# Products of q, k, v and gate for token blocks 1 to 3 over 64 rows, each row group in its own order of tiles, with another lead, first block and end

## The chip, the cores and the metric

The kernel runs on one core of a Trainium2 chip. Five engines with queues of their own take part: TensorE (in the profile PE, its weight loads PEld), VectorE (DVE), ScalarE (ACT), GpSimd (POOL) and SyncE (SP, which here only issues DMAs). The metric is device time in microseconds (us) of one launch; lower is better.

## The reference

The input x has 2048 tokens of 640 features. The output mixes two sublayers by a gate of each token: a Fourier mixing over features and tokens, and an attention with 32 query heads of 20 features and one head of keys and values (MQA). Everything is float32.

```python
a = einsum("bsd,ed->bse", x, dft_hid_re)
b = einsum("bsd,ed->bse", x, dft_hid_im)
y = einsum("ts,bse->bte", dft_seq_re, a) - einsum("ts,bse->bte", dft_seq_im, b)
q = heads(x @ wq)          # 32 heads of 20
k, v = x @ wk, x @ wv      # one head
o = softmax(q @ k.T * 20 ** -0.5) @ v
g = sigmoid((x * gate_w).sum(-1))
out = g * y + (1 - g) * (o @ wo)
```

## The kernel before

**Precision.** A float32 operand is split into a high part of type fp32r (by ACT) and the rest as a low part (by DVE or POOL). A product is three: high by high, high by low, low by high (`mm3`, L120).

**First stage, L347 to L503.** Tokens come in four blocks of 512, transposed: x is 640 rows, in five chunks of 128. `split_x1(n, c)` (L371) makes xh and xl of block n, chunk c, by one ACT and one DVE instruction. For each block five q tiles of 128 rows (m) take 15 products each (5 chunks by 3 terms, `q_mm`, L381), and one tile for k, v and the gate takes ten (`kv_mm`, L395): 85 products of 128 rows and 512 columns. `q_out` (L386) evicts a q tile: qh by ACT, ql by DVE, two DMAs on SP's queue to `qh_d` and `ql_d`. Its buffers qh and ql have three places each. `kv_out` (L402) evicts k and v: kvl by ACT, kvT by DVE, kh by ACT, kl by DVE, and six DMAs by POOL's queue into `ks`. `kv_turn` (L417) transposes kvT on TensorE into `vsb` and `gz`. `load_qs0` (L156) reads q of the first pair of heads back from HBM into `qs[0]`, by SP's queue.

Block 0 goes chunk by chunk as its data lands, with all six sums open (L438 to L456). Then stand the splits of block 1 (L460), the evictions of block 0 (L461 to L463) and the loads of block 2. Blocks 1 to 3 (L469 to L503) go tile by tile, and after 13 of the q tiles (`slots`) stand four a products.

**a, b and av.** For each pair of heads an a product (`a_unit`, L243) of 60 rows gives scores of 128 queries by 512 keys; DVE reduces each to a row maximum (L258). Two a products, one of each head, lie on rows 0 to 59 and 64 to 123 (`hh`), so that they can run side by side. `a_final` (L277) writes the negated maxima to HBM and reads them back into rows 60 and 61 of `qs`, after so many steps of a clock that `tick` counts (`later`). A b product of 62 rows (`b_unit`, L968) then gives scores less the maximum, transposed; ACT takes the exponential (pt), and `av_step` (L985) sums pt with v and a column of ones, in bank V.

**Lead and main loop.** `f_stream` gives the products of the Fourier part, 64 rows at a time; `Halves` (L779) keeps one queue for each half of the rows. The lead (from L1086) runs 120 of its steps, with a products spread over them until 40 pairs are done. Then plans, written out by hand, interleave Fourier steps (y0, y1), a, b, evictions (E) and av (V). The first plan, FIRST (L1084), has four more b products than AB15, just ahead of its two V: b products are one step ahead of av from there on.

**End.** `finish_last` (L1014) evicts the last av sums, spreads the softmax sums over the rows with a product by `spread`, takes the reciprocals, scales and splits. `begin_late` (L752) begins the output products of the last token tile with the chunks that are ready; `o_group` (L758) does the rest, and one DMA for each of the last eight token tiles stores 320 KB.

**Order.** TensorE, ACT, DVE and POOL run their instructions as the program lists them (`manual_schedule`); only SP's are put in order by the framework. A DMA that ACT or POOL issues stands in that engine's order.

## Time and profile before

| | us |
|---|---|
| median of 3 runs | 1720.98 (1719.69 to 1721.21) |
| the profiled execution | 1719.39 |
| its span | 1717.6 |
| PE busy | 1705.2 (99%) |
| DVE busy | 1380.8 (80%) |
| ACT busy | 1251.4 (73%) |
| POOL busy | 1117.4 (65%) |

The profile has one execution, instruction by instruction. Its span goes from the first to the last instruction of the program; 1.8 us of the execution's time lie around it. A row of the timeline has the start, the duration, the engine, the line, the operation, what is written and read, and, where the engine was idle ahead of it, for how long and what ended that. A matmul's duration includes the way through the array, so that back-to-back matmuls overlap; their starts tell the pace. Rows of a merged run of like instructions have their count (x5) and the time from the first start to the last end.

### The profile page before, as it was taken

The page shows a single profiled execution, that of the slowest core. Times are in us where ns is not written, and L with a number is a line of the kernel's source. Part 1 is how long each engine was busy: PE and PEld are TensorE (multiplying, and loading weights), DVE is VectorE, ACT ScalarE, POOL GpSimd, SP SyncE. Part 2 cuts the span into 40 slices and gives each one's busy share as a digit, 9 for nine tenths or more (in the row PEclk, how much of TensorE's full clock was granted, in tenths as well). Part 3 has the DMA queues.
Part 4 walks back from the last instruction along what each step waited for, and adds up shares of the span by engine and source line. Part 5 has one row for each costly group of instructions (what it writes and reads, how often), then busy time and mean ns, then how long its engine had stood idle before and what let it go on. Part 6 is the DMA issues. An engine that isn't in the chain of part 4 may idle for free.

```text
span 1717.6 us, 43365 instructions
## 1 busy us (share of the span) xinstructions
PE 1705.2 (99%) x16754; PEld 1235.0 (72%) x16754; DVE 1380.8 (80%) x2294; ACT 1251.4 (73%) x2547; POOL 1117.4 (65%) x947
## 2 busy tenths in 40 slices
PE   9999999999999999999999999999999999999998
PEld 7686777777777777777777777777777777777665
DVE  5788888888888888888888888888888888888823
ACT  4247888888776777777777777777777767678896
POOL 2354556332366568758767888888877765547786
PEclk9999999999999999999999999999999999999999
DMA  8641223222265546546666776655555533143332
GB/s 283 187 140 48 73 83 105 76 78 74 78 218 168 190 150 210 161 148 216 219 219 205 236 234 232 193 191 181 178 174 170 155 114 114 52 128 111 108 92 97
DMA packets 180394, 261.47 MB, mean 152 GB/s; under 512 B 35856, under 2 KB 134416, under 8 KB 180188
## 3 DMA queue, kind: packets, MB, share of 16 engines
q1 hardware_dynamic: 179420, 257.71, 46.9%
q8 instruction: 132, 2.16, 0.5%
q0 software_dynamic: 768, 0.99, 0.3%
q14 instruction: 74, 0.61, 0.1%
HBM read 184.42 MB, written 76.99 MB: 152 GB/s over the span
## 4 chain that ended last, share of the span: by engine, by line
PE 98%; ACT 1%; DVE 1%; issue 0%; DMA 0%; POOL 0%; SPq 0%; DVEq 0%; ACTq 0%
PE av L983 27%; PE y_p L791 21%; PE b L971 19%; PE a L251 15%; PE ab L791 7%; PE oo L791 3%; PE q L122 1%; PE q L124 1%; PE q L123 1%; PE kv L400 1%; ACT pt L979 1%; DMA wraw<-in_wq_dram 0%; DVE pt L1028 0%; DVE osp L1034 0%; POOL tb L808 0%
## 5 line engine op out<-in xcount | busy, mean ns | idle before, releaser
L258 DVE TENSOR_REDUCE mx<-a 128x1 f32<-128x512 f32 x2048 | 1304.4, 686 | 242.7 <-PE a L251 190.2
L979 ACT ACTIVATE pt<-b 128x512 f32<-128x512 f32 x2048 | 1058.0, 623 | 342.4 <-PE a L251 255.9
L971 PE MATMUL b<-qs,ks 62*128 62x512 f32 x2048 | 756.8, 408 | 1.9 <-ACT pt L979 1.4
L251 PE MATMUL a<-ks,qs 60*128 60x512 f32 x2048 | 703.4, 407 | 1.3 <-DVE mx L258 1.3
L791 PE MATMUL y_p<-tb,ch 64*128 64x320 f32 x3584 | 618.4, 307 | 0.0
L791 PEld LDWEIGHTS y_p<-tb,ch 64*128 64x128 f32 x3584 | 504.8, 186 | 3.0
L983 PE MATMUL av<-pt,vsb 128*32 128x512 f32 x4096 | 484.9, 597 | 0.0
L971 PEld LDWEIGHTS b<-qs,ks 62*128 62x128 f32 x2048 | 346.2, 184 | 186.4 <-DVE mx L258 124.7
L791 PE MATMUL y_p<-tb,cl 64*128 64x320 f32 x1792 | 455.0, 306 | 0.0
L251 PEld LDWEIGHTS a<-ks,qs 60*128 60x128 f32 x2048 | 345.0, 185 | 14.5 <-issue 3.2
L791 PEld LDWEIGHTS y_p<-tb,cl 64*128 64x128 f32 x1792 | 297.2, 185 | 2.6
L983 PEld LDWEIGHTS av<-pt,vsb 128*32 128x32 f32 x4096 | 111.4, 109 | 239.6 <-issue 230.0
L551 POOL TENSOR_TENSOR cl<-craw,ch 128x1024 fp32r<-128x1024 f32 x112 | 268.5, 2397 | 9.0
L833 POOL TENSOR_TENSOR yt<-yt,yu 128x320 f32<-128x320 f32 x86 | 75.0, 872 | 291.0 <-ACT yu L828 257.3
L833 POOL TENSOR_TENSOR abt<-abt,abu 128x320 f32<-128x320 f32 x64 | 55.8, 871 | 194.9 <-ACT abu L828 176.7
L545 POOL TENSOR_TENSOR craw<-craw 128x1024 f32<-128x1024 f32 x64 | 153.6, 2399 | 0.0
L550 POOL CAST ch<-craw 128x1024 fp32r<-128x1024 f32 x112 | 116.5, 1040 | 6.4 <-PE ab L791 2.3
L791 PE MATMUL oo<-wo,osp 64*128 64x320 f32 x816 | 91.6, 306 | 0.0
L791 PEld LDWEIGHTS oo<-wo,osp 64*128 64x128 f32 x816 | 86.5, 185 | 1.6
L577 POOL TENSOR_TENSOR tb<-braw,tb 128x320 fp32r<-128x320 f32 x80 | 69.8, 878 | 0.0
L791 PE MATMUL ab<-wbh,xh 64*128 64x320 f32 x256 | 59.5, 307 | 0.0
L791 PE MATMUL ab<-wbh,xl 64*128 64x320 f32 x256 | 59.4, 305 | 0.0
(140 smaller groups left out, 1619.8 us busy)
## 6 DMA issues: line engine op xcount, KB each, us to landing
craw<-in_cre_dram SPq DMA_DIRECT2D x80, 512.0 KB
craw<-in_cim_dram SPq DMA_DIRECT2D x64, 512.0 KB
s_d<-craw SPq DMA_DIRECT2D x32, 512.0 KB
craw<-s_d SPq DMA_DIRECT2D x32, 512.0 KB
braw<-b_d SPq DMA_DIRECT2D x80, 160.0 KB
xraw<-in_xT_dram SPq DMA_DIRECT2D x32, 320.0 KB
b_d<-abt SPq DMA_DIRECT2D x64, 160.0 KB
t_d<-braw SPq DMA_DIRECT2D x64, 160.0 KB
```

The source lines that it names most:

```text
L122: nc.tensor.matmul(ps, wh, xh, start=(i == 0), stop=False)
L251: nc.tensor.matmul(ps, qs[v][b : b + 60, qb * P : (qb + 1) * P], ks[b : b + 60, c * ROW : (c + 1) * ROW], start=True, stop=True,)
L258: nc.vector.tensor_reduce(mx[v][:, hh, qb, c : c + 1], ps, axis=AX.X, op=ALU.max)
L545: nc.gpsimd.tensor_tensor(x, raw[0], x, op=how)
L550: nc.gpsimd.tensor_copy(h, x)
L551: nc.gpsimd.tensor_tensor(l, x, h.bitcast(F32), op=ALU.subtract)
L577: nc.gpsimd.tensor_tensor(t[:, 1], raw, t[:, 0].bitcast(F32), op=ALU.subtract)
L791: nc.tensor.matmul(ps, w, x, start=start, stop=stop)
L833: nc.gpsimd.tensor_tensor(t0, t0, t1, op=ALU.add)
L971: nc.tensor.matmul(ps, ks[b : b + 62, kc * P : (kc + 1) * P], qs[NPAIR * (qc // 2) + p][b : b + 62, (qc % 2) * ROW : (qc % 2 + 1) * ROW], ...
L979: nc.scalar.activation(t, ps, AF.Exp, scale=SCALE)
L983: nc.tensor.matmul(ps[32 * g : 32 * g + 32, :], vsb[:, kc, :], t, start=first, stop=last)
```

## The change

- **Blocks 1 to 3.** Each product of 128 rows becomes two of 64 rows, on rows 0 to 63 and 64 to 127 (`RG`). Both halves add into the same bank, but at different times: rows 0 to 63 go through the tiles as kv, q1, q0, q2, q3, q4, rows 64 to 127 as q0, kv, q3, q4, q1, q2. `Tile.run` issues one product. When a tile's first half is complete, ACT copies one column of its last weights onto itself, and the tile's second half, which runs through the products in reverse, starts with those weights. When the tile is complete it is evicted in place. Loads, splits and transposes stand at numbered steps (`event`). Pairs of a stand at 30 steps, in place of 13 groups of four products. Low parts of x of blocks 2 and 3 are made by POOL.
- **First block.** The first chunk of wq comes in two pieces by ACT's DMA queue. The k/v products run a chunk behind q, and each tile is evicted when its last product has been issued.
- **qs[0].** For blocks 0 and 1 the first q tile is copied into `qs[0]` straight from qh and ql by six DMAs of POOL's queue; `load_qs0` is gone.
- **Lead.** a products start eight steps later; four b products stand at steps 102 to 117, in bank V; the first plan is AB15. The maxima come back after 3 ticks instead of 5 in this stage.
- **End.** The sums are turned by small products, inverted as 8 columns in place of 256, widened, and spread by products with the identity; `begin_late` is cut in pieces between these. The last token tile is stored in two halves, one by SP, one by ACT.

The old body of `finish_last` and the old loop over blocks 1 to 3 are in the listing above and are left out here.

```diff
-    spread = const.tile([P, P], F32, name="spread")
-    for g in range(0, P, 32):
-        nc.gpsimd.tensor_copy(spread[:, g : g + 32], ident[:, g + DH : g + DH + 1].to_broadcast([P, 32]))
...
-    def load_qs0(n):
-        if n == 0:
-            qs[0] = qbuf[0]
-        ts = slice(n * ROW, (n + 1) * ROW)
-        for hh in range(2):
-            r = slice(hh * DH, (hh + 1) * DH)
-            for k, src in enumerate((qh_d, qh_d, ql_d)):
-                b = 64 * hh + 20 * k
-                move(qs[0][b : b + 20, ts], src[r, ts])
...
-            later(5, move, qs[v][r : r + 2], m_d[v][:, hh * QB : (hh + 1) * QB].rearrange("i b g t -> i (b g t)"))
+            later(5 if stage["loop"] else 3, move, qs[v][r : r + 2], m_d[v][:, hh * QB : (hh + 1) * QB].rearrange("i b g t -> i (b g t)"))
...
-                nc.vector.tensor_tensor(xl[:, c], xs[n, c], xh[:, c].bitcast(F32), op=ALU.subtract)
-
-        def q_mm(ps, n, m, c):
+                low = nc.vector if n < 2 else nc.gpsimd
+                low.tensor_tensor(xl[:, c], xs[n, c], xh[:, c].bitcast(F32), op=ALU.subtract)
+
+        def q_ops(n, m):
             ms = slice(m * P, (m + 1) * P)
+            return [(P, w[:, c, ms], x[:, c]) for c in range(KC) for w, x in q_terms(n)]
+
+        def q_terms(n):
             xh, xl = xsp[n]
-            mm3(ps, wqh[:, c, ms], wql[:, c, ms], xh[:, c], xl[:, c], KC, c)
+            return (wqh, xh), (wqh, xl), (wql, xh)
+
+        def kv_ops(n):
+            xh, xl = xsp[n]
+            ops = [[(105, kvgs[:, c, :105], xh[:, c]), (41, kvgs[:, c, :41], xl[:, c])] for c in range(KC)]
+            ops[-1].reverse()
+            return sum(ops, [])
+
+        class Tile:
+
+            def __init__(self, ops, name, out):
+                self.ops, self.name, self.out = ops, name, out
+                self.ps, self.made = None, 0
+
+            def run(self, rows, i):
+                if self.ps is None:
+                    self.ps = rots[0](self.name)
+                if rows is not None and self.made >= len(self.ops):
+                    i = len(self.ops) - 1 - i
+                m, w, x = self.ops[i]
+                n = len(self.ops) if rows is None else 2 * len(self.ops)
+                self.made += 1
+                r = slice(0, P) if rows is None else RG[rows]
+                nc.tensor.matmul(self.ps[:m], w[r], x[r], start=self.made == 1, stop=self.made == n)
+                if self.made == n:
+                    self.out(self.ps)
+                elif rows is not None and self.made == len(self.ops):
+                    nc.scalar.activation(w[:, :1], words(w[:, :1]), AF.Copy)
+
+        def q_tile(n, m):
+            return Tile(q_ops(n, m), f"q_{n}_{m}", lambda ps: q_out(ps, n, m))
+
+        def kv_tile(n):
+            return Tile(kv_ops(n), f"kv_{n}", lambda ps: kv_out(ps, n))
 
         def q_out(ps, n, m):
...
+            if m == 0 and n < 2:
+                if n == 0:
+                    qs[0] = qbuf[0]
+                for hh in range(2):
+                    for k, src in enumerate((qh, qh, ql)):
+                        b = 64 * hh + 20 * k
+                        nc.gpsimd.dma_start(words(qs[0][b : b + 20, ts]), words(src[hh * DH : (hh + 1) * DH]))
...
-            return kvT
+            kvTs[n] = kvT
...
+        kvTs = {}
+        arot = Rot(["S2", "S3", "S4"])
+
         load_x1(0, 0)
-        move(kvg, wkvg.rearrange("(c p) n -> p c n", p=P))
-        pkv = rot("kv_0")
-        pq = [rot(f"q_0_{m}") for m in range(KC)]
-        for c in range(KC):
-            if c:
-                load_x1(0, c)
+        cut = 2 * P
+        pieces = (slice(0, cut), slice(cut, D))
+        raw0 = w1.tile([P, D], F32, name="wraw", bufs=2)
+        for cs in pieces:
+            nc.scalar.dma_start(raw0[:, cs], wq_v[:, 0, cs])
+        split_x1(0, 0)
+        for cs in pieces:
+            split(raw0[:, cs], wqh[:, 0, cs], wql[:, 0, cs])
+        for c in range(1, KC):
+            load_x1(0, c)
             raw = raw_tile([P, D], "wraw") if c in (2, 3) else w1.tile([P, D], F32, name="wraw", bufs=2)
             move(raw, wq_v[:, c])
-            if c == 0:
+            if c == 1:
+                move(kvg, wkvg.rearrange("(c p) n -> p c n", p=P))
+            split_x1(0, c)
+            split(raw, wqh[:, c], wql[:, c])
+            if c == 1:
                 nc.vector.tensor_copy(kvgs[:, :, :41], kvg)
                 nc.vector.tensor_tensor(
                     kvgs[:, :, 64:105], kvg, kvgs[:, :, :41].bitcast(F32), op=ALU.subtract
                 )
-            split_x1(0, c)
-            split(raw, wqh[:, c], wql[:, c])
-            kv_mm(pkv, 0, c)
-            for m in range(KC):
-                q_mm(pq[m], 0, m, c)
+        rots = [rot]
+        tkv = kv_tile(0)
+        tq = [q_tile(0, m) for m in range(KC)]
+        order = [[(k, m) for m in range(KC) for k in range(3)] for c in range(KC)]
+        order[0] = [(0, 0), (0, 1), (1, 0), (1, 1), (0, 2), (0, 3), (0, 4), (2, 0), (2, 1), (1, 2), (1, 3), (1, 4)]
+        order[0] += [(2, 2), (2, 3), (2, 4)]
+        for c in range(KC):
+            ops = [(t, 3 * c + k) for k, m in order[c] for t in tq[m : m + 1]]
+            kv = [(tkv, i) for i in range(max(0, 2 * c - 2), 2 * c + 2 if c == KC - 1 else 2 * c)]
+            for t, i in kv[:2] + ops[:6] + kv[2:] + ops[6:]:
+                t.run(None, i)
         for c in range(KC):
             load_x1(1, c)
         for c in range(KC):
             split_x1(1, c)
-        kvT = kv_out(pkv, 0)
-        for m in range(KC):
-            q_out(pq[m], 0, m)
         for c in range(KC):
             load_x1(2, c)
-        load_qs0(0)
...
+        rots[0] = Rot(["F1", "V", "S0", "F0", "S1"])
+        at = {}
+
+        def event(k, f, *args):
+            at.setdefault(k, []).append((f, args))
+
+        NB = 17 * KC
         for n in range(1, 4):
+            s0 = (n - 1) * NB
+            for c in range(KC):
+                if n == 1:
+                    event(s0, load_x1, 3, c)
+                if n < 3:
+                    event(s0 + 12 + 14 * c, split_x1, n + 1, c)
             if n > 1:
+                event(s0, lambda n=n: load_w(n - 2, 0, x1.tile([P, KC, ROW], F32, tag="xr", name="wraw")))
+                event(s0 + 40, split_w, n - 2)
+            event(s0 + 50, kv_turn, n)
+        s0 = 2 * NB
+        for k in range(2):
+            event(s0 + 25, load_x, k)
+            event(s0 + 55 + 15 * k, split_x, k)
+        event(s0 + 70, load_x, 2)
+        event(32, kv_turn, 0)
+        event(s0 + 50, gate_out)
+        slots = [40 + 7 * k for k in range(24)] + [220 + 6 * k for k in range(6)]
+
+        for n in range(1, 4):
+            ts = [kv_tile(n)] + [q_tile(n, m) for m in (1, 0, 2, 3, 4)]
+            rows = [[(ts[z], i) for z in x for i in range(len(ts[z].ops))] for x in (range(6), (2, 0, 4, 5, 1, 3))]
+            for i, both in enumerate(zip(*rows, strict=True)):
+                k = NB * (n - 1) + i
+                for f, args in at.pop(k, ()):
+                    f(*args)
+                if k in slots:
+                    for hh in range(2):
+                        a_half(hh, arot.tags[arot.n % 3])
+                        arot.n += 1
+                for r, (t, j) in enumerate(both):
+                    t.run(r, j)
+        assert not at
...
-    def begin_late(e):
-        ps = begun[NT - 1, e] = bank(f"S{e}", f"o_late{e}")[:, :HALF]
+    def begin_late(e, c0, c1):
+        if c0 == 0:
+            begun[NT - 1, e] = bank(f"S{e}", f"o_late{e}")[:, :HALF]
+        ps = begun[NT - 1, e]
         h, l = osp[NT - 1]
-        for c in range(OC):
+        for c in range(c0, c1):
             mm3(ps, h[:, c], l[:, c], *wos[c, e], OC + 1, c)
 
...
+        if tb == NT - 1:
+            at = (nc.sync, nc.scalar)[e]
+            at.dma_start(out[tb * P : (tb + 1) * P, e * HALF : (e + 1) * HALF], t)
+        elif e == 1:
             move(out[tb * P : (tb + 1) * P].rearrange("p (e n) -> p e n", e=2), acc[tb])
...
+        HC = ROW // 2
         a = av[1]
+        ob = [pp.tile([P, ROW], F32, name="pt")[:, :HC] for _ in range(2)]
+        on = [pp.tile([P, ROW], F32, name="pt")[:, :HC] for _ in range(2)]
+        rec = [op.tile([P, 16], F32, name="rc")[:, :8] for _ in range(2)]
+        wide = [pp.tile([P, ROW], F32, name="pt")[:, :HC] for _ in range(2)]
+        nc.scalar.activation(ob[0], a[:, :HC], AF.Copy)
+        nc.vector.tensor_copy(ob[1], a[:, HC:])
+        pick4 = ident.rearrange("p (g x) -> p g x", x=32)[:, :, DH]
+        for i in range(2):
+            ps = bank(f"S{3 + i}", f"turned{i}")
+            for c in range(2):
+                nc.tensor.matmul(ps[:, 4 * c : 4 * c + 4], ob[i][:, c * P : (c + 1) * P], pick4, start=True, stop=True)
+            nc.vector.reciprocal(rec[i], ps[:, :8])
+            nc.vector.tensor_copy(
+                wide[i].rearrange("p (k x) -> p k x", x=32),
+                rec[i].rearrange("p (k o) -> p k o", o=1).to_broadcast([P, 8, 32]),
+            )
+        begin_late(0, 0, 2)
         h, l = last_hl
+        for i, low in enumerate(((nc.vector, nc.gpsimd), (nc.vector, nc.vector))):
+            ps = bank("S2" if i == 0 else "V", f"wide{i}")
+            for c in range(2):
+                nc.tensor.matmul(ps[:, c * P : (c + 1) * P], wide[i][:, c * P : (c + 1) * P], ident, start=True, stop=True)
+            nc.vector.tensor_tensor(on[i], ob[i], ps[:, :HC], op=ALU.mult)
+            begin_late(0, 2 + i, 3 + i)
+        begin_late(1, 0, OC)
+        for i, low in enumerate(((nc.vector, nc.vector, nc.gpsimd, nc.gpsimd), (nc.vector, nc.vector, nc.gpsimd, nc.vector))):
+            cs = slice(i * HC, (i + 1) * HC)
             for j in range(2):
                 for g in NEW[j]:
+                    nc.scalar.activation(h[g : g + DH, j, cs], on[i][g : g + DH], AF.Copy)
+                for k, g in enumerate(NEW[j]):
+                    low[2 * j + k].tensor_tensor(
+                        l[g : g + DH, j, cs], on[i][g : g + DH], h[g : g + DH, j, cs].bitcast(F32), op=ALU.subtract
                     )
 
...
-    FIRST = AB15[:-2] + "b0S3 b1S0 b0S2 b1S3 V V".split()
-
     LEAD = 8
     NL = 2 * (UV + LEAD)
     KL = 15 * SJ
+    LATE = 8
+    EARLY_B = {102: (0, 0), 107: (1, 0), 112: (0, 1), 117: (1, 1)}
     done = first = 2 * state[0]
     for n in range(1, KL + 1):
         y_put(1)
         for g in range(2):
             halves.run(g)
-        while done < first + (NL - first) * n // KL:
+        while done < first + (NL - first) * max(0, n - LATE) // (KL - LATE):
             if done % 2 == 0:
                 tick()
             a_half(done % 2)
             done += 1
+        if n in EARLY_B:
+            hh, qc = EARLY_B[n]
+            b_unit(0, hh, 0, qc, "V")
...
-        yield FIRST
+        yield AB15
...
-    made = 0
-    old = []
+    made = 1
+    old = STEPS[:1]
...
-    for e in range(2):
-        begin_late(e)
```

More of the change, by code (lines that the diff above doesn't have):

```diff
@@ L393, in q_out @@
             move(ql_d[ms, ts], ql)
-        def kv_mm(ps, n, c):
-            xh, xl = xsp[n]
-            end = c == KC - 1
-            for high in (not end, end):
-                m, x = (105, xh) if high else (41, xl)
-                nc.tensor.matmul(ps[:m], kvgs[:, c, :m], x[:, c], start=(c == 0 and high), stop=(end and high))
+            if m == 0 and n < 2:
[5 more added lines that the diff above has]
+                        nc.gpsimd.dma_start(words(qs[0][b : b + 20, ts]), words(src[hh * DH : (hh + 1) * DH]))
         def kv_out(ps, n):
@@ L414, in kv_out, with kv_turn @@
                     nc.gpsimd.dma_start(words(ks[r0 + 20 * k : r0 + 20 * k + 20, ts]), words(src))
-            return kvT
-        def kv_turn(kvT, n, rot):
-            ps = rot(f"kvt_{n}")
+            kvTs[n] = kvT
+        def kv_turn(n):
+            kvT = kvTs.pop(n)
+            ps = arot(f"kvt_{n}")
             for j in range(4):
@@ L460 @@
             split_x1(1, c)
-        kvT = kv_out(pkv, 0)
-        for m in range(KC):
-            q_out(pq[m], 0, m)
         for c in range(KC):
             load_x1(2, c)
-        load_qs0(0)
-        rot = Rot(["F1", "V", "S0", "F0"])
-        slots = {1: (2, 3, 4), 2: range(KC), 3: range(KC)}
-        for n in range(1, 4):
-            if n == 1:
-                for c in range(KC):
-                    load_x1(3, c)
-            if n > 1:
-                load_w(n - 2, 0, x1.tile([P, KC, ROW], F32, tag="xr", name="wraw"))
-            pkv = rot(f"kv_{n}")
-            for c in range(KC):
-                kv_mm(pkv, n, c)
-            kvT, kvT0 = kv_out(pkv, n), kvT
-            if n == 3:
-                for k in range(2):
-                    load_x(k)
-            for m in range(KC):
-                ps = rot(f"q_{n}_{m}")
-                for c in range(KC):
-                    q_mm(ps, n, m, c)
-                split_x1(n + 1, m)
-                if n > 1 and m == 1:
-                    split_w(n - 2)
-                q_out(ps, n, m)
-                if (n, m) == (1, 0):
-                    load_qs0(1)
-                if m == slots[n][0]:
-                    kv_turn(kvT0, n - 1, rot)
-                if m in slots[n]:
-                    for z in range(4):
-                        a_half(z % 2, f"S{1 + z}")
-                if (n, m) == (3, 1):
-                    kv_turn(kvT, 3, rot)
-                    gate_out()
-                if n == 3 and m in (2, 3):
-                    split_x(m - 2)
-                if (n, m) == (3, 3):
-                    load_x(2)
@@ L1014, in finish_last @@
     def finish_last():
-        ob = op.tile([P, ROW], F32, name="ob")
-        cols = [slice(0, ROW // 2), slice(ROW // 2, ROW)]
+        HC = ROW // 2
         a = av[1]
-        nc.scalar.activation(ob[:, cols[0]], a[:, cols[0]], AF.Copy)
-        nc.vector.tensor_copy(ob[:, cols[1]], a[:, cols[1]])
-        sums = []
-        for i, cs in enumerate(cols):
-            sums.append(bank(f"S{2 + i}", f"sums{i}")[:, cs])
-            nc.tensor.matmul(sums[i], spread, ob[:, cs], start=True, stop=True)
@@ L1025, in finish_last @@
-        r, on = [pp.tile([P, ROW], F32, name="pt") for _ in range(2)]
-        h, l = last_hl
-        for cs, ps, low in zip(cols, sums, ((nc.vector, nc.gpsimd), (nc.vector, nc.vector))):
-            nc.vector.reciprocal(r[:, cs], ps)
-            nc.vector.tensor_tensor(on[:, cs], a[:, cs], r[:, cs], op=ALU.mult)
+        ob = [pp.tile([P, ROW], F32, name="pt")[:, :HC] for _ in range(2)]
+        on = [pp.tile([P, ROW], F32, name="pt")[:, :HC] for _ in range(2)]
+        rec = [op.tile([P, 16], F32, name="rc")[:, :8] for _ in range(2)]
@@ L1030, in finish_last @@
+        for i, low in enumerate(((nc.vector, nc.vector, nc.gpsimd, nc.gpsimd), (nc.vector, nc.vector, nc.gpsimd, nc.vector))):
+            cs = slice(i * HC, (i + 1) * HC)
             for j in range(2):
                 for g in NEW[j]:
-                    nc.scalar.activation(h[g : g + DH, j, cs], on[g : g + DH, cs], AF.Copy)
-                for g in NEW[j]:
-                    low[j].tensor_tensor(
-                        l[g : g + DH, j, cs], on[g : g + DH, cs], h[g : g + DH, j, cs].bitcast(F32), op=ALU.subtract
+                    nc.scalar.activation(h[g : g + DH, j, cs], on[i][g : g + DH], AF.Copy)
+                for k, g in enumerate(NEW[j]):
+                    low[2 * j + k].tensor_tensor(
+                        l[g : g + DH, j, cs], on[i][g : g + DH], h[g : g + DH, j, cs].bitcast(F32), op=ALU.subtract
```

1 line of the change is left out of this document (removed).

## Prediction

> **What bounds the kernel now.** I read the page's span and its chain of work first, then the busy time by stage, then the timeline of each seam between stages.
>
> ```profile
> span 1717.6 us, 43365 instructions
> ...
> PE 98%; ACT 1%; DVE 1%; issue 0%; DMA 0%; POOL 0%; SPq 0%; DVEq 0%; ACTq 0%
> ```
>
> The chain that ended last is TensorE's own work, so a change counts where it alters TensorE's work or makes it wait. The windows below hold: the first token block, blocks 1 to 3, the lead, the first plan up to its first av product, the main loop, and the end (each row: length; busy time and count of PE, PEld, DVE, ACT, POOL; granted clock; DMA share; GB/s).
>
> ```profile
> 5.94:26.39 20.45, 20.33 (x85) 15.54 (x86) 12.12 (x19) 11.05 (x19) 0.71 (x1) 1.00 0.95 318
> 26.39:98.13 71.74, 71.74 (x325) 50.80 (x324) 53.18 (x91) 21.13 (x41) 26.09 (x34) 1.00 0.65 208
> 98.13:120.90 22.77, 21.48 (x269) 20.95 (x266) 20.79 (x36) 10.20 (x25) 15.40 (x16) 1.00 0.42 134
> 120.90:128.69 7.79, 6.78 (x55) 4.64 (x51) 6.11 (x10) 6.97 (x16) 4.27 (x6) 1.00 0.27 86
> 128.69:1698.20 1569.51, 1568.52 (x15935) 1127.91 (x15934) 1275.49 (x2118) 1192.99 (x2433) 1059.63 (x871) 1.00 0.47 148
> 1698.20:1712.73 14.53, 12.24 (x76) 11.24 (x76) 11.55 (x20) 6.78 (x15) 6.82 (x9) 1.00 0.24 91
> ```
>
> The main loop, 1570 us, keeps its plans apart from the first, and starts with 40 pairs of a done in both kernels. The change is worth what the other stages give.
>
> **Blocks 1 to 3: what the row groups remove.** TensorE's timeline around one group of a products (start, duration):
>
> ```profile
> 44.02 0.39 PE L124 MATMUL q<-xh,wql 128*128 128x512 f32 x1
> 44.34 0.73 PE L251 MATMUL a<-ks,qs 60*128 60x512 f32 x4
> 45.00 0.50 PE L122 MATMUL q<-xh,wqh 128*128 128x512 f32 x1
> 45.34 0.39 PE L123 MATMUL q<-xl,wqh 128*128 128x512 f32 x1
> 45.57 0.40 PE L124 MATMUL q<-xh,wql 128*128 128x512 f32 x1
> ```
>
> Product follows product after 0.233 us (45.34 to 45.57). From 44.02 to 45.34 run one q product, two pairs of a over 64 rows side by side, and one q product: 4 x 0.233 = 0.93 us of work in 1.32. The other 0.39 lies in four starts 0.32 to 0.34 apart, two on each side of the change of shape. Thirteen such groups (52 a products) make 5.1 us. As a check, 255 products x 0.233 + 26 pairs x 0.233 + four sets of transposes of about 0.25 = 66.5 us, and the window has 71.7.
>
> After the change all products there use 64 rows, so nothing changes shape: **-5.1**. The products do not get cheaper: each matmul becomes two of 64 rows, which by the a pairs take one product's time. Thirty a pairs are placed there instead of 26: **+0.9**, which the lead gets back.
>
> The Trainium skill, "TensorE: Matmul & The Clock Gate", section "Part 1: The HAM clock gate", gives back-to-back products as N/2.4 GHz + 2.5 ns, 215.7 ns for 512 columns. This trace has 0.233 us at granted clock 1.00; were the page's figure to hold for the new pairs alone, an estimate of 255 x 0.017 = 4.3 us more would go. The trace has a duration for both shapes, so the sum uses 0.233.
>
> What is late next here is DVE, whose reduction frees the banks of the a products:
>
> ```profile
> L258 DVE TENSOR_REDUCE mx<-a 128x1 f32<-128x512 f32 x48 | 29.7, 680 | 0.0
> ```
>
> A pair costs two reductions, some 1.3 us. Now three banks rotate and a pair comes every 7 steps, 8 x 0.233 = 1.86 us; its second bank is the first bank of the pair before, free 1.15 us after that one's start. DVE may thus be 0.7 late. It is later where an eviction stands ahead of the reductions: at k/v of block 2 it waits for kvl (0.6), makes kvT (0.7), waits for kh (0.6), makes kl (0.7), about 2.4 us past its turn, so TensorE waits 1.7. At q0 of block 1 I get 0.35, at the pairs of q evictions 0.1 to 0.5 each, at the gate and the transposes together 0.8. Sum **+3.9** (bounds +1 and +6). The one-column ACT copies between a tile's halves find 5 steps or more (1.2 us) and cost nothing, unless ACT is that late.
>
> **The seam from block 0 to block 1: what is added.** Now block 1 starts without a gap:
>
> ```profile
> 26.16 0.40 PE L124 MATMUL q<-xh,wql 128*128 128x512 f32 x1
> 26.39 0.40 PE L400 MATMUL kv<-xh,kvgs 128*105 128x512 f32 x1
> ```
>
> It can, because x of block 1 was split long before, ahead of block 0's evictions on ACT and DVE, whose instructions run as the program lists them:
>
> ```profile
> 16.24 2.70 ACT L378 ACTIVATE xh<-xr 128x512 fp32r<-128x512 f32 x5
> ```
>
> ```profile
> 17.11 3.09 DVE L379 TENSOR_TENSOR xl<-xr,xh 128x512 fp32r<-128x512 f32 x5
> ```
>
> In the changed program a tile evicts itself when its last product is issued, so block 0's evictions come ahead of `split_x1(1, c)` (L460) on both queues. What these cost:
>
> ```profile
> 24.44 0.63 ACT L410 ACTIVATE kh<-kvT 20x512 fp32r<-20x512 f32 x1 [0.75 <-DVE kvT L409]
> 25.09 1.58 ACT L390 ACTIVATE qh<-q 128x512 fp32r<-128x512 f32 x3
> 28.67 0.60 ACT L390 ACTIVATE qh<-q 128x512 fp32r<-128x512 f32 x1 [2.00 <-PE kv L400]
> ```
>
> The fourth qh waits here although its product is long done: qh has three buffers, and the first is still being written out, by the SP DMA below, 25.72 to 28.67. After the change that buffer is also read by POOL's copies into qs[0], six in place of `load_qs0`:
>
> ```profile
> 25.72 0.82 SPq L114 DMA_DIRECT2D qh_d<-qh  x2
> ```
>
> ```profile
> 25.68 0.73 POOL L414 DMA_DIRECT2D ks<-kh  x1 [20.77 <-ACT qh L390]
> 26.41 0.52 POOL L414 DMA_DIRECT2D ks<-kl  x1
> ```
>
> ```profile
> ks<-kh POOLq DMA_DIRECT2D x16, 40.0 KB, 3.2
> ks<-kl POOLq DMA_DIRECT2D x8, 40.0 KB, 4.0
> ```
>
> Let E be the time at which block 1 could start. q0's last product is 15 products before E: its sum is out at E-3.1, qh0 at E-2.5. POOL issues six copies at about 0.5 each from E-2.2; the fifth, the last that reads qh0, at E-0.1, landing 3.2 to 4.0 later, near E+3.5; the sixth reads ql0, is issued at E+0.4 and lands near E+4.4. Then ACT: qh3, qh4, five xh at 0.54 (2.70/5). DVE: ql3 from about E+4.6, ql4, five xl at 0.61 (3.09/5), the last done at E+8.9. Block 1's k/v tile uses one chunk of x every two steps; its step 8 needs the last xl and could run at E+1.9 (8 x 0.233). So TensorE is late by **+7.1**. If the buffers were free at once, kh, kl, the three evictions and the splits alone give E+5.9, +4.1: the lower bound. Behind POOL's copies stand block 0's k/v copies, needed only by the a products at step 40. An idle stretch of 5 us brings the clock in:
>
> ```profile
> 1712.70:1715.30 2.60, 0.03 (x1) 0.00 (x0) 0.72 (x2) 0.00 (x0) 0.28 (x1) 1.00 1.02 390
> 1715.40:1717.60 2.20, 0.00 (x0) 0.00 (x0) 0.00 (x0) 0.00 (x0) 0.00 (x0) 0.50 0.33 127
> ```
>
> 2.6 us after the last product the granted clock is 0.50. Most of a slow stretch would hide behind DVE's 0.61 per chunk; I take **+0.5** (0 to 2).
>
> **Start and block 0.** Now ACT waits for x, then for all of wq's first chunk:
>
> ```profile
> 2.01 0.22 ACT L108 ACTIVATE gate<-ident 128x16 f32<-128x16 f32 x1
> 4.45 0.63 ACT L378 ACTIVATE xh<-xr 128x512 fp32r<-128x512 f32 x1 [2.22 <-DMA xr<-in_xT_dram]
> 5.75 0.74 ACT L117 ACTIVATE wqh<-wraw 128x640 fp32r<-128x640 f32 x1 [0.67 <-DMA wraw<-in_wq_dram]
> ```
>
> After, two pieces come by ACT's queue, issued after 2.23; the first, 128 KB, should land between 5.0 and 6.2, so the first product starts near 5.65 and later pieces cost some 0.7. Against 5.94 with 20.45 - 85 x 0.233 = 0.65 of waits: **-0.4** (-1.2 to +0.6). Dropping `spread` frees POOL, which nobody waits for.
>
> **Lead and first plan.** The lead's first wait and the end of the first plan:
>
> ```profile
> 100.29 0.49 PE L251 MATMUL a<-ks,qs 60*128 60x512 f32 x1 [1.26 <-DVE mx L258]
> ```
>
> ```profile
> 126.15 1.48 PE L971 MATMUL b<-qs,ks 62*128 62x512 f32 x3
> 128.27 0.49 PE L971 MATMUL b<-qs,ks 62*128 62x512 f32 x1 [0.65 <-ACT pt L979]
> 128.69 1.92 PE L983 MATMUL av<-pt,vsb 128*32 128x512 f32 x16
> ```
>
> The a wait (1.5) goes, as `LATE` holds a back, but the lead's first sum now lies in S0, which block 3's last q tile gives up only after ql: 1.45. Together **0**. Ten a pairs instead of 14: **-0.9**. The four b products at the end, 2.5 us paced by ACT, move into the lead; there they cost 0.5 of TensorE, and, all in bank V behind an ACT that is 45% busy (10.20 of 22.77) and itself waits for evictions, some 1.0 of waiting: **-1.0** (-2.2 to +0.5). The shorter delay of the maxima's write-back, 3 ticks, leaves the DMA over 8 us before the first b.
>
> **End.**
>
> ```profile
> 1698.63 1.16 PE L1024 MATMUL sums<-ob,spread 128*128 128x256 f32 x4 [0.47 <-ACT ob L1019]
> ```
>
> ```profile
> 1708.06 0.42 PE L122 MATMUL o<-wl,osp 128*128 128x320 f32 x1 [1.26 <-DVE acc L774]
> ```
>
> ```profile
> 1708.54 5.40 SPq L114 DMA_DIRECT2D out_dram<-acc  x8
> ```
>
> ```profile
> 1709.40:1716.20 6.80, 3.33 (x23) 3.06 (x21) 3.01 (x6) 1.59 (x3) 3.49 (x4) 0.94 1.00 386
> ```
>
> Four products of sums become 16 small ones (about 0.2 each by 1.16/4, +2.4), and the waits of 0.8 and 1.4 before o products go: TensorE ends as before. But from 1709.4 the DMA engines are full: 8 x 320 KB at 386 GB/s last 6.8 us, so the end follows the first store. Its POOL sum comes some 0.8 earlier, as POOL and ACT are done with the splits earlier: **-0.8** (-1.8 to +0.3). The halved last store adds nothing while the engines are full.
>
> **Sum**: -0.4 + 7.1 + 0.5 - 5.1 + 0.9 + 3.9 + 0 - 0.9 - 1.0 - 0.8 = +4.2 us on the profiled execution (1719.4 = span 1717.6 + 1.8 around it): 1723.6. The median of the runs is 1.6 above that execution, so I forecast **1725.2**.
>
> **Rivals.**
> - *The seam is short* (0.25): the buffers of qh do not hold ACT, and the seam costs the bound of 4.1 without a slow clock: 1725.2 - 3.5 = 1721.7. For it: without POOL's copies the first qh would be free by E+0.5. Against: the 28.67 row shows ACT waiting for just this buffer.
> - *The seam is hidden* (0.13), the other side: x of block 1 is split before TensorE needs it, at E+1.9 or earlier, because ACT and DVE run the splits ahead of the evictions. The seam's 7.6 go, and with DVE less late half of 3.9: 1715.7. Against: the 16.24 row stands ahead of the evictions just as the program has it.
> - *The clock falls and stays down* (0.12): two slow stretches of about 3.4 us behind the idle seam, so that products beyond the DVE-paced ones run at half pace: +2 to +3 instead of 0.5, 1727.5. The Trainium skill, same page and section, has such a rule: an idle window of about 3.4 us halves the clock, a busy one restores it; the two clock rows agree with its first half, and no row here has a gap inside the kernel to show the second.
> - *The row groups do not run side by side* (0.02): 255 x 0.233 = 59 us more, 1784. The a pairs speak against it.
>
> **Numbers.** Forecast 0.45, other small mixtures 0.03. The measurement tells about 0.2% (3.4 us) from no change; 1724.4 lies just under the forecast, so I give a fifth of the forecast to "same". Slower 0.54, same 0.34, faster 0.12. Range 1717.5 to 1730: from the hidden seam without further gain to +9, the seam with a slow clock and DVE at its upper bound.
>
> **What would show it.** After: a gap of TensorE of 6 to 8 us behind block 0, ended by DVE's xl, with qh3 waiting for a copy by POOL; no starts 0.33 apart from there to the lead; a wait of 1 to 2 us for DVE's mx after k/v of block 2; no run of b products ahead of the first av; first store some 0.8 earlier relative to the last av. Wrong if the splits of block 1 stand ahead of the evictions, or if pairs of 64 rows take other than 0.233.

## The result and the profile after

The changed kernel takes **1745.4 us** (median of 4 runs, 1744.2 to 1748.2) where the kernel before takes 1721.1 beside it: 1.0147 times (95% interval 1.0134 to 1.016). Slower was the likeliest sign of the forecast, but 1725.2 was the forecast and 1730 the end of its range. The head of the page, then the chain that ended last:

```profile
span 1743.1 us, 43923 instructions
...
PE 93%; issue 1%; ACT 1%; POOL 1%; DMA 0%; DVE 0%; DVEq 0%; ACTq 0%; POOLq 0%
```

TensorE's share of the chain fell from 98% to 93%: it now waits on the way that sets the end. The windows by stage show where (start, block 0, seam, blocks 1 to 3, lead with first plan, main loop, end; columns as in the prediction):

```profile
0.00:14.41 14.41, 4.21 (x18) 3.92 (x19) 0.71 (x2) 2.54 (x4) 3.59 (x11) 0.81 0.84 279
14.41:36.54 22.13, 22.13 (x85) 17.08 (x85) 9.04 (x15) 7.30 (x13) 2.15 (x4) 0.89 0.40 126
36.54:43.59 7.05, 0.16 (x1) 0.00 (x1) 2.19 (x4) 2.60 (x6) 4.08 (x9) 0.73 0.85 275
43.59:127.24 83.65, 74.15 (x586) 64.56 (x586) 57.31 (x95) 24.73 (x60) 38.66 (x44) 0.94 0.49 161
127.24:155.09 27.85, 26.59 (x310) 25.18 (x310) 18.56 (x31) 16.85 (x38) 18.83 (x19) 1.00 0.44 143
155.09:1725.26 1570.17, 1569.27 (x15936) 1128.42 (x15934) 1277.11 (x2120) 1194.02 (x2433) 1060.43 (x871) 1.00 0.47 148
1725.26:1743.10 17.84, 12.67 (x88) 12.35 (x88) 10.00 (x22) 6.88 (x15) 7.95 (x10) 1.00 0.39 148
```

Set against the rows of before (5.94; 20.45; none; 71.74; 22.77 + 7.79 = 30.56; 1569.51; and 19.4 from the last av product to the span's end): +8.5, +1.7, +7.0, +11.9, -2.7, +0.7, -1.6. That is the whole difference of the spans, +25.5. What TensorE waited for up to the lead, by the view of waits (us in total, times, longest):

```profile
PE q L398 <- ACT wqh L114: 8.9, 1, 8.9
PE kv L398 <- ACT xh L365: 6.9, 1, 6.9
PE a L238 <- DVE mx L245: 4.5, 3, 1.6
PE a L238 <- DMA ks<-kh: 1.9, 1, 1.9
PE a L238 <- DMA qs<-ql: 1.5, 1, 1.5
PE ab L838 <- DVE ql L415: 1.2, 1, 1.2
PE kv L398 <- DVE xl L367: 0.4, 1, 0.4
```

The same view of before, blocks 0 to 3, has a single wait of 0.5. (The wait of the warm-up products for their operand, 1.3 in both kernels, is left out.)

**The start.** ACT's timeline of the first 16 us:

```profile
2.01 0.22 ACT L105 ACTIVATE gate<-ident 128x16 f32<-128x16 f32 x1
7.79 1.99 ACTq L471 DMA_DIRECT2D wraw<-in_wq_dram  x2
9.83 0.63 ACT L365 ACTIVATE xh<-xr 128x512 fp32r<-128x512 f32 x1 [7.61 <-DMA xr<-in_xT_dram]
13.94 0.42 ACT L114 ACTIVATE wqh<-wraw 128x256 fp32r<-128x256 f32 x1 [3.48 <-DMA wraw<-in_wq_dram]
14.93 0.52 ACT L114 ACTIVATE wqh<-wraw 128x384 fp32r<-128x384 f32 x1 [0.57 <-DMA wraw<-in_wq_dram]
```

ACT is free at 2.23, but issues the first piece of wq only at 7.79 and the second within the two microseconds behind it. The bracket at 9.83 names the load of x, which had landed at 4.39: xh stands behind the two issues in ACT's order, and it was they that were held. By the semaphore events of the trace, SP's and ACT's transfers count on eight semaphores in turn, and ACT's first issue waits for the one that SP's fourth transfer had taken; that landed at 7.77. ACT's second issue waits in the same way for SP's sixth, which landed at 9.43.

**The seam.** ACT's timeline between block 0 and block 1:

```profile
36.80 0.60 ACT L414 ACTIVATE qh<-q 128x512 fp32r<-128x512 f32 x1
39.73 0.60 ACT L414 ACTIVATE qh<-q 128x512 fp32r<-128x512 f32 x1 [2.34 <-DMA qh_d<-qh]
42.42 0.60 ACT L414 ACTIVATE qh<-q 128x512 fp32r<-128x512 f32 x1 [2.10 <-DMA qh_d<-qh]
42.92 2.70 ACT L365 ACTIVATE xh<-xr 128x512 fp32r<-128x512 f32 x5
```

The two last qh wait for a buffer, and block 1's five xh stand behind them. By the semaphore events the fourth qh waits for SP's write of the second (issued at 35.27, landed at 39.63), and the fifth for SP's write of the third (issued at 37.42, landed at 42.32).

**The clock.** The windows over its three stretches at 0.50, behind the start, behind the seam and behind the wait for k of block 3:

```profile
9.06:19.30 10.24, 4.89 (x12) 3.83 (x13) 4.91 (x9) 5.42 (x10) 0.00 (x0) 0.50 0.89 312
39.78:50.02 10.24, 6.06 (x27) 5.46 (x29) 4.39 (x7) 4.46 (x9) 1.15 (x3) 0.50 0.65 212
114.88:118.29 3.41, 3.41 (x20) 3.08 (x18) 2.81 (x7) 1.03 (x3) 2.80 (x4) 0.50 0.00 0
```

At 0.50 product follows product after 0.427 us instead of 0.233. Twelve products of block 0 pay 0.194 each, 2.3 us (block 0 grew by only 1.7, since the kernel before waits 0.65 in it); 4.84 us of block 1 (45.20 to 50.04) hold 2.2, the last stretch 1.5.

### The profile page after: what moved, and what is told of

The parts are those of the page before. It is cut to its first block, busy times and chain, and to the rows that moved or that the text cites. A ratio compares the mean times of both kernels' runs of the same rounds, so it can differ in the third digit from the quotient of the medians.

```text
span 1743.1 us, 43923 instructions
## 1 busy us (share of the span) xinstructions
PE 1709.2 (98%) x17021; PEld 1251.5 (72%) x17021; DVE 1374.9 (79%) x2286; ACT 1254.9 (72%) x2566; POOL 1135.7 (65%) x966
## 4 chain that ended last, share of the span: by engine, by line
PE 93%; issue 1%; ACT 1%; POOL 1%; DMA 0%; DVE 0%; DVEq 0%; ACTq 0%; POOLq 0%
PE av L1030 27%; PE y_p L838 21%; PE b L1018 18%; PE a L238 15%; PE ab L838 8%; PE oo L838 3%; PE q L398 1%; ACT pt L1026 0%; DMA qs<-ql 0%; POOL xl L367 0%; DMA ks<-kh 0%; POOL ks L438 0%; POOL w0l L199 0%; PE kv L398 0%; PE o L119 0%
## 5 line engine op out<-in xcount | busy, mean ns | idle before, releaser
L238 PEld LDWEIGHTS a<-ks,qs 60*128 60x128 f32 x2048 | 349.9, 185 | 21.0 <-DVE mx L245 8.8
L398 PE MATMUL q<-xh,wqh 64*128 64x512 f32 (+1 forms) x175 | 56.6, 414 | 8.9 <-ACT wqh L114 8.9
```

The lines of the kernel that those rows point to most:

```text
L238: nc.tensor.matmul(ps, qs[v][b : b + 60, qb * P : (qb + 1) * P], ks[b : b + 60, c * ROW : (c + 1) * ROW], start=True, stop=True,)
L398: nc.tensor.matmul(self.ps[:m], w[r], x[r], start=self.made == 1, stop=self.made == n)
```

## The experiments

The ratios are to the kernel before, run beside it on the same chip, with the 95% interval. The first table's four kernels tell the start and the seam apart; each edit is to the changed kernel.

**Pieces by SP** (e1).

```diff
-            nc.scalar.dma_start(raw0[:, cs], wq_v[:, 0, cs])
+            nc.sync.dma_start(raw0[:, cs], wq_v[:, 0, cs])
```

> The two pieces of wq's first chunk are issued by SP, between the load of x and what followed it, instead of by ACT; nothing else differs from the changed kernel. Theory (ACT's issue of them is held by a DMA semaphore that SP's fourth transfer holds until 7.77, and the xh behind it on ACT is held too): the first product starts at 6.0 to 6.8 instead of 14.41 and block 0, no longer cold, takes 20.5 instead of 22.1: 8 + 1.6, about 1736 (1734 to 1738). Rival (the start is lost to the transfers of wq and x as such, all of which must land anyway): the first product starts early but block 0 waits later for its chunks, the end of block 0 moves by under 3 us: 1742 to 1745.

**Splits first** (e2): tiles of block 0 that are complete go to a list.

```diff
-                    self.out(self.ps)
+                    late.append(self) if rows is None else self.out(self.ps)
...
             split_x1(1, c)
+        for t in late:
+            t.out(t.ps)
```

> Block 0's six evictions are emitted behind the splits of block 1's x, as in the kernel before; nothing else differs from the changed kernel. Theory (the order of evictions and splits on ACT and DVE makes the seam): the 7.05 us gap at 36.5 goes, and with it the half clock from 39.8 to 50.0 (some 1.6): about 1737 (1735.5 to 1739.5). Rival (the qh buffers and POOL's copies into qs hold the evictions anyway and come back as waits for banks in block 1): only the clock and a part of the gap, 1740 to 1743.

**Both** (e3).

> Both edits together: pieces by SP, splits of block 1 ahead of block 0's evictions. If the start (about 9.5) and the seam (about 8.7) are separate losses they add: about 1727 (1725 to 1730). If both are paid for by one thing, the half clock or the transfers, the sum falls short: 1732 or more. What then is left over the kernel before, some 6 us, must lie in blocks 1 to 3 (waits for mx and for POOL's copies).

**Pieces by ACT, issued first** (e8).

```diff
-    nc.scalar.activation(gate, ident[:, :NT], AF.Exp)
...
-        load_x1(0, 0)
...
             nc.scalar.dma_start(raw0[:, cs], wq_v[:, 0, cs])
+        nc.scalar.activation(gate, ident[:, :NT], AF.Exp)
+        load_x1(0, 0)
```

> The pieces stay on ACT's queue, but ACT issues them as its first work, ahead of the load of x by SP and of ACT's Exp, so that both take DMA semaphores nobody has used. Theory (the issue was held by a shared DMA semaphore): issued before 1.5, landed by 5.5, first product at 5.5 to 6.5, about 1736 (1734 to 1738), as with the pieces on SP. Rival (ACT's queue itself gets few bytes while SP's queue is full): landing after 8, first product after 9, 1739 to 1744.

| | us | ratio | first product | block 1 starts | lead starts |
|---|---|---|---|---|---|
| before | | 1 | 5.94 | 26.39 | 98.13 |
| changed | 1745.4 | 1.0147 (1.0134 to 1.016) | 14.41 | 43.59 | 127.24 |
| e1 | 1734.7 | 1.0081 (1.0066 to 1.0096) | 5.31 | 33.77 | 118.15 |
| e2 | 1739.0 | 1.0103 (1.0086 to 1.012) | 13.93 | 35.95 | 122.49 |
| e3 | 1727.7 | 1.0045 (1.003 to 1.006) | 5.51 | 26.27 | 114.10 |
| e8 | 1736.4 | 1.0091 (1.0076 to 1.0106) | 6.25 | 35.82 | 118.25 |

All four times lie in the range that the first theory of each had given. Two details differ: e1's first product came at 5.31 and not at 6.0 to 6.8, and e2 kept one stretch of half clock behind block 0 (42.27 to 45.68). In e8 ACT's rows at the start are:

```profile
0.72 0.90 ACTq L469 DMA_DIRECT2D wraw<-in_wq_dram  x2
...
5.26 0.63 ACT L364 ACTIVATE xh<-xr 128x512 fp32r<-128x512 f32 x1 [2.09 <-DMA xr<-in_xT_dram]
5.79 0.40 ACT L113 ACTIVATE wqh<-wraw 128x256 fp32r<-128x256 f32 x1
6.48 0.52 ACT L113 ACTIVATE wqh<-wraw 128x384 fp32r<-128x384 f32 x1 [0.28 <-DMA wraw<-in_wq_dram]
```

The same two transfers by the same queue land some 8 us earlier; 7.1 of that is the issue, which waits for nothing. So ACT's queue as such was not the loss; the late issue was. And the losses add: e1 gains 10.7, e2 6.4, both together 17.7.

In the traced executions e2 and e3 give something back, though: blocks 1 to 3 of e3 take 87.83 where the changed kernel's take 83.65. (This execution of e3, 1731.5, is the longest of its four; the others took 1727.0 to 1728.1 at a higher mean granted clock, 0.998 to 0.999 against 0.996, so they lost less to the clock.) TensorE's waits of e3 up to the lead:

```profile
PE a L238 <- DVE mx L245: 4.7, 3, 1.7
PE kv L398 <- ACT kvgs L402: 3.8, 1, 3.8
PE a L238 <- DMA ks<-kh: 1.8, 1, 1.8
PE a L238 <- DMA qs<-ql: 1.4, 1, 1.4
PE ab L841 <- DVE ql L415: 1.2, 1, 1.2
```

The second is new. It is the one-column copy that ACT makes between the halves of a tile: with block 0's evictions now ahead of it in ACT's order, it waits with them for buffers of qh. The prediction had named this as the case in which the copies cost.

**Warm-up to the first product** (e4): the idle start filled, to see the clock's price alone.

```diff
-    for _ in range(9):
+    for _ in range(34):
```

> The changed kernel with 34 instead of 9 passes of the warm-up products, which fill TensorE's idle start up to the first product at 14.4; nothing else differs. Theory (the granted clock falls to 0.50 after an idle stretch, and block 0's products at 0.427 instead of 0.233 us are the 1.7 us by which block 0 is longer): clock 1.00 throughout block 0, which takes 20.5 instead of 22.1: about 1743.7 (1742.5 to 1744.5). Rival (block 0 is longer because its transfers land later, whatever the clock): no change, 1745.4.

1745.2 us, 1.0148 (1.013 to 1.0166): no gain. The clock did stay at 1.00 in block 0, which took 21.03 instead of 22.13 (of 1.6 expected, 1.1 came). But the lead starts only 1.1 earlier (126.15) and the span ends 0.2 earlier: blocks 1 to 3 take 84.87 instead of 83.65. The half clock of the seam now reaches from 38.30 to 48.54, behind a first product at 41.28, and so covers 7.3 us of block 1 instead of 6.4, which is 0.4 of the 1.2. The other 0.8 is in the waits of these blocks, which by the view of waits sum to 10.3 instead of 9.5. So the price in block 0 is seen, but no run shows that the whole kernel can have it back.

**Lead and end alone** (e5): the kernel before with the changed `finish_last`, `begin_late`, last store, lead and first plan; nothing of blocks 0 to 3.

> The kernel before with only the changed lead and first plan (a pairs held back by 8, four b products in the lead) and the changed end; blocks 0 to 3 and the start are those of before, so the lead has 14 pairs of a where the changed kernel has 10. If the lead and the end are gains of their own: lead and first plan -1.8 (of the 2.7 of the changed kernel, less 4 pairs), end -1.6: about 1717.6 (1716.5 to 1719). Rival (the lead's gain is only that four pairs were moved to the blocks): the end alone, 1719.4 to 1720.

1716.9 us, 0.9984 (0.9975 to 0.9994), as expected, though not for the reason expected. Lead with first plan, and end, of this run:

```profile
98.24:127.48 29.24, 27.82 (x321) 25.69 (x317) 25.44 (x43) 16.69 (x39) 18.88 (x19) 1.00 0.40 128
1698.15:1715.80 17.65, 12.69 (x89) 12.36 (x88) 10.00 (x22) 6.87 (x15) 8.63 (x10) 0.99 0.39 149
```

The lead gains 1.3, the end 1.7. But the main loop of this execution (1570.7) is 1.2 longer than that of before, as it is by 0.3 to 1.5 in the other kernels here, all of which have the changed lead; its av products fall behind by small steps all through it, and at no one place. All are set against one execution of before, so it stays open whether the lead's gain is given back there or that execution had a short loop. Only the end's gain is shown.

**The waits of blocks 1 to 3** (e6, e7). e6 is e3 with block 0's evictions spread and four buffers for qh; e7 also moves the pairs of a. A step is one product as two halves of 64 rows; blocks 1 to 3 have 85 each, counted from 0.

```diff
-        for t in late:
+        for t in late[:2]:
             t.out(t.ps)
...
+        for k, t in zip((10, 15, 19, 25), late[2:]):
+            event(k, t.out, t.ps)
...
-            qh = x1.tile([P, ROW], F32R, tag="qh", name="qh", bufs=3)
+            qh = x1.tile([P, ROW], F32R, tag="qh", name="qh", bufs=4)
```

> As with both edits before (pieces by SP, splits first), and two waits of blocks 1 to 3 taken away: block 0's evictions of q1 to q4 are spread over steps 10 to 25 of block 1, so that the one-column copy between the halves of the k/v tile doesn't stand behind all of them on ACT; and qh has four buffers instead of three. Theory (ACT in order: the copy waits 3.9 behind evictions, and the qh that waits for a buffer being written out holds DVE's ql and the reductions at steps 96 and 180, 1.9 and 1.7): these 7.5 go, and two of the three windows of half clock behind them, 1.5 each: 1727.7 - 10 = about 1717.5 (1716 to 1721). Rival (DVE's throughput is what the a pairs wait for): the waits for mx stay, only the 3.9 and one window go, 1722 to 1723.

```diff
-        slots = [40 + 7 * k for k in range(24)] + [220 + 6 * k for k in range(6)]
+        slots = [40, 46, 52, 58, 78, 93, 99, 105, 119, 125, 131, 137, 143, 149, 161, 167, 178, 184, 190, 204, 210, 216, 222, 228, 234, 240, 246, 252]
```

> As the run before it, and 28 pairs of a instead of 30, at steps where neither an eviction on DVE nor a copy by POOL is under way (none within some 9 steps behind the end of a tile, the fifth pair at step 78 instead of 68, the first that needs k of block 3 at 234 instead of 220). Theory (the remaining waits are for the place of a pair, not for DVE's total work): the waits at steps 68, 117 and 220 (1.7, 1.7, 2.1) and the window of half clock behind the last go, two pairs more in the lead cost 1: 6 less than the run before it, about 1711.5 (1710 to 1715). Rival (DVE as a whole is full): the waits come back at other pairs, 0 to 2 less.

Both missed: 1725.7 (1.0026, 1.0013 to 1.0038) and 1725.5 (1.0035, 1.0022 to 1.0049). Of the waits expected to go, five were gone in e7 (at the copy between the halves, at steps 68, 96 and 117, and for k at 220); the one near step 180 stayed, and others came, which at first looks like the rival, DVE as a whole being full. But e7's timelines, of ACT in block 1 and of DVE in block 3, name waits of another kind:

```profile
28.70 0.20 ACT L402 ACTIVATE kvgs<-kvgs 128x1 fp32r<-128x1 f32 x1 [4.50 <-PE kv L398]
28.93 0.59 ACT L432 ACTIVATE kvl<-kv 41x512 f32<-41x512 f32 x1
```

```profile
79.68 0.69 DVE L415 TENSOR_TENSOR ql<-q,qh 128x512 fp32r<-128x512 f32 x1 [2.56 <-DMA ql_d<-ql]
80.29 2.47 DVE L245 TENSOR_REDUCE mx<-a 128x1 f32<-128x512 f32 x4
...
91.83 1.34 DVE L457 TENSOR_SCALAR gz<-gz 128x16 f32<-128x16 f32 x1
```

First, block 0's tiles were complete in the order q0, q1, k/v, so that my edit left k/v for step 10: ACT sat idle for 4.5 us at the copy that waits for TensorE, with k/v's eviction, whose sum was long done, behind it, and the first pair of a waited for k. Second, with four qh the next to run out is ql: DVE idles 2.6 us until SP's write of the old one is done, and four reductions follow. Third, the gate's operations stand on DVE just ahead of the pair at step 228, which waits 2.4. All three are places in an order; whether these or DVE's throughput cost the time is what the next two runs ask.

**All of them** (e9, and e10 with the pairs at the changed kernel's steps). To e7:

```diff
-        for t in late[:2]:
-            t.out(t.ps)
+        for z in (0, 2, 1):
+            late[z].out(late[z].ps)
...
-        for k, t in zip((10, 15, 19, 25), late[2:]):
+        for k, t in zip((10, 11, 15), late[3:]):
...
-            ql = x1.tile([P, ROW], F32R, tag="ql", name="ql", bufs=3)
+            ql = x1.tile([P, ROW], F32R, tag="ql", name="ql", bufs=4)
...
-            kl = x1.tile([DH, ROW], F32R, name="kl")
+            kl = x1.tile([DH, ROW], F32R, name="kl", bufs=1)
...
-        rots[0] = Rot(["F1", "V", "S0", "F0", "S1"])
+        rots[0] = Rot(["F1", "V", "S1", "F0", "S0"])
...
-        event(s0 + 50, gate_out)
...
         assert not at
+        later(6, gate_out)
```

> As the run with moved pairs before (28 pairs, placed), with the waits that its trace still shows taken away: block 0's evictions in the order q0, k/v, q1 ahead of block 1 and q2 to q4 right behind the copy between the halves of the k/v tile; four buffers for ql too (one for kl); the gate's five operations moved from block 3 into the lead; the banks of blocks 1 to 3 in another order, so that the lead's first sums lie in banks long free. Theory (row groups save about 4 us over blocks 1 to 3, 71.7 to 67.5, and everything above that is waits for ACT, DVE and POOL in order, with a window of half clock behind two of them): waits of 2.3 (ks), 0.7, 1.8, 2.6, 0.9 and 1.4 and two windows of 1.6 go, 1725.5 - 12.9 = 1712.6 (1711 to 1717), faster than the kernel before. Rival (DVE as a whole is the bound of blocks 1 to 3, as it has 60 reductions of 0.68 and the evictions to do there): at most half of it, 1719 or more.

> As the run beside it, but with the 30 pairs of a at the changed kernel's own steps. If the place of the pairs matters once the buffers are free, the waits at steps 68, 117 and 220 are still there (1.7, 1.7, 2.1, and a window of 1.6), less the two pairs that the lead then hasn't to do: 1717 to 1720. If it doesn't, no more than 1 above the run beside it.

e9 takes **1714.8 us, 0.9968 (0.9955 to 0.998)**: faster than both kernels. Its block 0 and blocks 1 to 3, and its only row of waits there:

```profile
5.49:25.90 20.41, 20.41 (x87) 15.56 (x86) 12.10 (x20) 10.19 (x17) 2.25 (x5) 1.00 0.94 309
25.90:95.38 69.48, 68.11 (x584) 63.86 (x584) 50.62 (x83) 23.38 (x57) 42.59 (x52) 1.00 0.62 211
```

```profile
PE a L238 <- DVE mx L245: 1.4, 4, 0.8
```

The clock is 1.00 throughout. Blocks 1 to 3 with row groups take 69.48 against 71.74, with 28 pairs of a against 26. e10 takes 1718.9 (0.9989, 0.998 to 0.9999), 4.1 more than e9. Its blocks 1 to 3 take 73.34, 3.9 more: two pairs more (0.5), and three waits at steps 68, 117 and 220 in the same view, 4.4 in place of 1.4:

```profile
PE a L238 <- DMA ks<-kh: 1.9, 1, 1.9
PE a L238 <- DVE mx L245: 1.5, 1, 1.5
PE a L238 <- DMA qs<-ql: 1.0, 1, 1.0
```

So the place of the pairs does matter once the buffers are free. And DVE's total work is not the bound: it is busy for 50.62 of e9's 69.48 us, and TensorE waits 1.4 for it, so the rival of e7 and e9 falls. e9 does relieve DVE a little, by four reductions (2.7) and by the gate, which moves to the lead; e10, which has all 60 reductions, waits 1.5 for DVE. Which of e9's other edits gives how much was not tested one by one.

## Why the prediction was wrong, step by step

| term of the prediction | predicted | measured |
|---|---|---|
| start and block 0 | -0.4 | +10.2 (8.5 and 1.7) |
| seam | +7.1 | +7.05 up to the first product, and 1.1 in the two steps behind it |
| clock behind the seam | +0.5 (0 to 2) | 2.2, and 1.5 behind the wait at 114.46 |
| mode switches, four more a pairs | -4.2 | -3.2, by e9: 69.48 - 1.4 of waits + 0.5 for two pairs - 71.74; -4.7 with these waits counted from start to start |
| DVE's reductions | +3.9 | 4.5 in three waits; 5.3 from start to start |
| POOL's copies into qs and ks | nothing | 3.4 in two waits; 4.2 from start to start |
| lead's first wait | 0 | 0 (1.2 for ql in place of 1.3 for mx) |
| lead's a pairs, early b products | -1.9 | -1.5: 27.85 - 30.56 + 1.2, the wait for ql that now lies ahead of the window |
| end | -0.8 | -1.6 |

The view counts a wait from the end of the product before, and a product lasts 0.39 with its way through the array. From start to start, less 0.233 a step, a wait costs more: in the changed kernel 1.9, 1.9, 1.8, 1.7 and 2.3 for the five waits of a pair, where the view has 1.5, 1.6, 1.5, 1.4 and 1.9, and 1.5 for the one ahead of the lead, where it has 1.2. With these, its blocks 1 to 3 add up: 285 steps of 0.233 and 1.0 of transposes are 67.4, and 11.1 of waits, 1.1 in the first two steps and 3.7 of half clock make 83.3 of the 83.65 measured.

- **The step that failed is "two pieces come by ACT's queue, issued after 2.23".** I took the row in which ACT comes free for the time of issue. The issue waited 5.6 us for a semaphore shared with SP's transfers, the pieces needed some 6 more in the traffic of that moment, and x's first split stood behind both. With the pieces on SP (e1) the first product starts at 5.31, and the term would have been about right. The time for the transfer itself, 2.8 to 4.0 from issue to landing, stands there without a row: e1's first piece took 3.5 (1.18 to 4.63), but e8's, by ACT's queue, 4.7 (0.72 to 5.41), and the changed kernel's 6.1.
- **The clock was under-sized.** It was priced at one seam, and there at 0.5 on the ground that DVE's pace would hide it; DVE held only the first two steps, and eleven steps ran at 0.427. The start that wasn't foreseen brought a second stretch, and a wait of 1.9 a third. The third rival, two slow stretches of 3.4 each, had the mechanism and +2 to +3 of it; the stretches of the start and the seam have three times 3.41 each. The prediction's own two clock rows, which it read as agreeing with an idle window of about 3.4 us, have the clock at 0.50 only 2.6 us behind the last product. The Trainium skill, "TensorE: Matmul & The Clock Gate", section "Part 1: The HAM clock gate", says that the window is free-running and lasts 3413 ns; the trace agrees with the length, as all stretches inside the span are multiples of 3.41 (10.24 is three).
- **The seam was right in its mechanism, and in its size partly by luck.** The gap comes from the order of evictions and splits, as e2 shows: without that order it is gone. The prediction had one qh wait for a buffer, for a copy by POOL; two wait, one behind the other (2.3 and 2.1), and for SP's writes, while the last copy by POOL that reads the first qh lands only at 41.01. Whether POOL's copies make SP's writes longer stays open. The second wait was not in the sum: the last xl is done at 47.11, 10.6 behind E (the time at which block 1 could start, here 36.54), and not 8.9. The gap came out at 7.05 all the same, since it ends with the first xh by ACT and not with the last xl by DVE; the rest shows as 1.1 in the first two steps and in the half clock.
- **"Behind POOL's copies stand block 0's k/v copies, needed only by the a products at step 40"** looked at block 0 and at its first pair. The pairs that first need q of block 1 (step 68) and k of block 3 (step 220) wait 1.5 and 1.9 for copies issued by POOL. That is the cover that wasn't there; moving the pairs takes both away (e9 has neither, e10 has both).
- **DVE's waits** had about the right sum, by luck in part. The one at k/v of block 2 was foreseen (1.7) and came (1.5, at 83.05). The two at steps 96 and 180 are not the "0.1 to 0.5" of a pair of q evictions: two tiles end together, the last of qh's three buffers is taken (in e7 ql's), and the reductions stand behind the eviction that waits. With four buffers of qh (e6) the wait at step 96 is gone.
- **Row groups and their gain** held. By the prediction's own paces e9's work is 255 + 28 steps of 0.233 and 1.0 of transposes, 66.9; with 1.4 of waits that is 68.3 of the 69.48 measured. The other 1.2 is the same difference in how a wait is counted: from start to start the four waits cost 0.6, 0.6, 0.6 and 1.1, in all 2.9, and 66.9 + 2.9 is 0.3 above the measured.
- **The end** gained twice the term: first store 8.6 behind the last av (1733.87) instead of 10.3:

```profile
1733.87 5.15 SPq L111 DMA_DIRECT2D out_dram<-acc  x7
1739.11 0.41 SPq L821 DMA_DIRECT2D out_dram<-acc  x1
```

Six rows of that table, the seam's by its gap, lie within the bounds given or within 1 us of the term. The start's +10.2 and the 3.4 for POOL's copies were in no range: the one was costed by when ACT is free and not by what its next instruction waits for, the other was put at nothing after a look at its first use alone. The clock's 2.2 and 1.5 together are outside their range (0 to 2) too.

## What to carry to other kernels

A DMA issue is an instruction that can wait: before moving one to a compute engine's queue, ask which semaphore and which buffer it needs, and what stands behind it on that engine. Where pieces of work are placed by hand, list for each engine what the instruction in front waits for; a busy share of 70% does not show that a queue is blocked by its head. A change that looks like a loss can hold a gain: here the row groups, lead and end were worth 0.3% once the waits around them were taken away (lead and end alone, e5, 0.16%).
